# One block's second matrix products run as two half-height streams that trade accumulator banks

## The chip, the cores and the metric

The kernel runs on one core of a Trainium2 chip. The metric is the device time of one execution in microseconds (us), as the median of several runs. Beside it stands one profiled execution, with the start and duration of every instruction on each engine: TensorE (PE, its weight loads listed apart as PEld), VectorE (DVE), ScalarE (ACT), GpSimd (POOL) and SyncE (SP), which here issues every DMA.

## The reference

A decayed causal attention without softmax makes the activations `x`; a feed-forward layer with a rational activation follows.

```python
scores = (1 / sqrt(D)) * q @ k^T              # 8 batches, 8 heads, 576 positions, D = 64
ret = scores * where(rel >= 0, gamma ** rel, 0)
x = (ret @ v) as [4608 tokens, 512]
h = x @ w_in                                  # w_in 512 x 2048
g = (a0 + a1 h + a2 h^2 + a3 h^3) / (1 + |b0| |h| + |b1| h^2 + 1e-6)
out = g @ w_out                               # w_out 2048 x 512
```

## The kernel before, in words

The tokens are cut into nine blocks `b` of 512, the 2048 hidden channels into sixteen parts `f` of 128. A step is one pair `(b, f)`; there are 144 of them, and blocks 2 to 8 run one after the other with f = 0 to 15. Values that enter TensorE are split into a high and a low part (`xhi`, `xlo`; `g[:, 0]`, `g[:, 1]`; `w[:, 0]`, `w[:, 1]`), and of the four products of two split numbers three are made.

In each step TensorE does two things. `gemm1` makes the hidden values `h` of one part: 12 products of a 128x128 stationary operand with 512 moving columns, into one accumulator bank. `gemm2` adds one part's contribution to the block's output: for each of four token groups `t` of 128 tokens, three products with `g[:, i, ts]` stationary and the 512 columns of `w[:, j, :]` moving, all contracting over the full 128 channels. The four groups have a bank each, in two tiles `accs[b]` of two banks (`t // 2` is the tile, `t % 2` the bank), open over the block's 16 parts. `gemm2` runs three steps behind `gemm1`, since between them ScalarE and VectorE work out the rational function (`ffn_p` to `ffn_q3`) and split it (`ffn_hi`, `ffn_lo`).

Every fourth step also holds a `visit`: the attention of one 128-token unit, in products of 64 rows by 64 columns on quarters of TensorE's array. Its two halves of the array's rows run as two streams (`emit`) that write different accumulator banks. Where a half comes to a bank that the other half wrote before, `follow` makes it wait: an empty instruction on SP waits for the earlier product, and the later product waits for that instruction. After a visit SP issues the two 512 KB loads of a later unit (`load_unit`: `qk`, then `kv`).

The order on each engine is the order in which the code is written out (`InOrder`): lists of names per step, of which `REST` holds for this part of the program. In it `visit` comes behind `gemm1`, and `gemm2` behind `visit`. All compute instructions carry the line number of the helper that records them. In block 4, the fifth, the visits fall in the steps of which `gemm2` does parts 3, 7, 11 and 15; that of part 15 of block 3 comes just ahead of it.

Of the kernel before, what the change touches and what calls it, by code (L numbers as in the profile page):

```python
# [21 lines left out]
P = 128  # L22
B, H, S, D = 8, 8, 576, 64
# [31 lines left out]

VISITS = {0: (4, 5), 2: (5, 6), 4: (6, 7), 6: (7, None), 23: (None, 8)}
FIRST_DENSE = 22
VISITS |= {24 + 2 * i: (8 + i, 9 + i) for i in range(3)}
VISITS |= {30 + 4 * i: (11 + i, 12 + i if i < 24 else None) for i in range(25)}
WARM = [8, 3, 2]  # L60
# [16 lines left out]
def retention_ffn(ctx: ExitStack, tc: tile.TileContext, qkv, w_in, w_out, ab, masks, gq, gv, out):  # L77
# [10 lines left out]
    nc = tc.nc  # L88
# [15 lines left out]
    pe, act, dve, pool = (InOrder(tc, e) for e in (nc.tensor, nc.scalar, nc.vector, nc.gpsimd))  # L104
# [187 lines left out]
    def follow(ins, earlier):  # L292
        how = mybir.DependencyInfo(mybir.DependencyClass.Sync, mybir.DependencyReason.DATA)
        tc.add_manual_dep(ins.ins, earlier.ins.name, how, reason="rows of the array that write one bank")
        return ins
# [85 lines left out]
    accs = {}  # L381
# [68 lines left out]
    def ffn_lo(b, f, by_pool):  # L450
# [4 lines left out]
        else:  # L455
            dve.tensor_tensor(g[:, 1, :], p, g[:, 0, :].bitcast(F32), ALU.subtract)

    def gemm2(b, f, first, last):
        if first:
            accs[b] = [ps_acc.tile([P, 2, DM], F32, tag="acc", name=f"acc{b}_{f}_{t}") for t in range(2)]  # L460
        g = gs.pop((b, f))
        w = parts[1, f]
        for t in range(4):
            ts = slice(t * P, (t + 1) * P)
            acc = accs[b][t // 2][:, t % 2, :]
            for k, (i, j) in enumerate(((0, 0), (0, 1), (1, 0))):
                pe.matmul(acc, g[:, i, ts], w[:, j, :], start=(first and k == 0), stop=(last and k == 2))
        if not last:
            return
        for t, acc in enumerate(accs.pop(b)):  # L470
            r0 = b * 512 + t * 256
            rows = out[r0 : r0 + 256, :].rearrange("(t p) d -> p t d", p=P)
            if b == 1:
                for j in range(2):
                    o = cnv.tile([P, DM], F32, tag="c", name=f"o{b}_{t}_{j}")
                    act.activation(o, acc[:, j, :], AF.Copy, scale=-1.0)
                    nc.sync.dma_start(rows[:, j, :], o)
                continue
            if b == 0 and f == NF - 1:
                o = part[t]  # L480
                dve.scalar_tensor_tensor(o, acc, -1.0, o, ALU.mult, ALU.add)
            else:
                o = op.tile([P, 2, DM], F32, tag=f"o{t}", name=f"o{b}_{t}_{f}")
                act.activation(o, acc, AF.Copy, scale=-1.0)
            if f < NF - 1:
                part.append(o)
            else:
                nc.sync.dma_start(rows, o)
# [4 lines left out]
    first = half + NF  # L493
# [77 lines left out]
    def products(i):  # L571
        nonlocal done
        while done < len(steps) and i - done >= lag(i):
            gemm2(*steps[done])
            done += 1

    for i in range(len(steps) + lag(len(steps))):
# [3 lines left out]
        if i in VISITS:  # L581
            a, k = VISITS[i]
# [13 lines left out]
        if i == half:  # L596
            ps = ps_at.tile([P, 2, 512], F32, tag="at", name="free_at")
            free_at.extend((ps[:, 0], ps[:, 1]))
        elif i == FIRST_DENSE - 1:
            free_at.clear()  # L600
# [43 lines left out]
```

## Time and profile before

| | |
|---|---|
| median of 3 runs | 940.39 us (940.2 to 940.61) |
| profiled execution, whole | 940.24 us |
| its span, first to last instruction | 938.5 us |
| PE busy | 899.4 us (96%), 7852 products |
| DVE busy | 825.0 us (88%) |
| ACT busy | 710.2 us (76%) |
| POOL busy | 153.0 us (16%) |
| DMA | 65.50 MB, mean 70 GB/s |

Products overlap in TensorE's pipeline: the duration listed for one with 512 columns is 0.39 us, while the next one starts 0.23 us after it. What one costs in a row of them is therefore read from the distance of starts. Where a row stands for several instructions, its duration runs from the first one's start to the last one's end. The names `acc`, `h`, `ps`, `y`, `qk` and `kv` in the profile are the tiles of the code.

### The profile page before, as it was taken

How to read it: one execution, taken by the hardware profiler on the slowest of the kernel's cores; microseconds unless marked ns; L12 is line 12 of the kernel's file. 1: busy time of each engine (PE TensorE's matmuls, PEld its weight loads, DVE VectorE, ACT ScalarE, POOL GpSimd, SP SyncE). 2: the span in 40 equal slices, each digit the busy share in tenths (PEclk: the TensorE clock that was granted, in tenths of full speed). 3: DMA queues.
4: the chain of work that ended last, by engine and by line, in shares of the span. 5: the costliest groups of instructions: out<-in, count | busy, mean ns of one | idle time of the engine just before them, and what ended most of it. 6: DMA issues, size and time to landing. Idle time of an engine off the chain costs nothing.

```text
span 938.5 us, 19369 instructions
## 1 busy us (share of the span) xinstructions
PE 899.4 (96%) x7852; PEld 737.2 (79%) x7852; DVE 825.0 (88%) x1252; ACT 710.2 (76%) x1274; POOL 153.0 (16%) x128
## 2 busy tenths in 40 slices
PE   6689889989999999999999999999999999999997
PEld 6567668877878888888888888888888888888886
DVE  3799999999888888888888999898888888888895
ACT  4567788887777777877787778777877787867775
POOL 3544344444100000000000000000000000000000
PEclk9789999989999999999999999999999999999999
DMA  9976000003212111211121112111211121001001
GB/s 341 362 276 203 1 0 1 1 13 124 91 46 87 49 36 32 84 40 41 43 90 45 47 46 91 45 47 46 90 46 46 45 91 47 1 1 45 1 1 45
DMA packets 20568, 65.50 MB, mean 70 GB/s; under 512 B 2432, under 2 KB 2432, under 8 KB 20480
## 3 DMA queue, kind: packets, MB, share of 16 engines
q1 hardware_dynamic: 20480, 64.28, 19.5%
q8 instruction: 61, 1.00, 0.4%
q14 instruction: 27, 0.22, 0.1%
HBM read 54.83 MB, written 9.44 MB: 68 GB/s over the span
## 4 chain that ended last, share of the span: by engine, by line
PE 46%; DVE 28%; ACT 20%; issue 4%; DMA 1%; POOL 0%; SPq 0%; DVEq 0%; ACTq 0%; POOLq 0%
PE h L73 21%; PE acc L73 20%; DVE p L73 14%; DVE v L73 7%; ACT u L73 6%; ACT v L73 4%; ACT g L73 3%; ACT kv L73 3%; DVE c L73 3%; ACT free_at L73 2%; PE psNone L73 2%; PE ps L73 2%; DVE qk L73 1%; DVE g L73 1%; DVE xlo L73 1%
## 5 line engine op out<-in xcount | busy, mean ns | idle before, releaser
L73 PE MATMUL acc<-w,g 128*128 128x512 f32 x1632 | 399.7, 394 | 5.5 <-ACT o L73 3.6
L73 PE MATMUL h<-xhi,w 128*128 128x512 f32 x1152 | 385.4, 396 | 15.9 <-DVE p L73 15.9
L73 PEld LDWEIGHTS acc<-w,g 128*128 128x128 f32 x1632 | 305.4, 189 | 72.3 <-ACT o L73 4.0
L73 PEld LDWEIGHTS h<-xhi,w 128*128 128x128 f32 x1152 | 219.3, 190 | 69.0 <-DVE p L73 23.0
L73 PE MATMUL h<-xlo,w 128*128 128x512 f32 x576 | 227.0, 394 | 0.0
L73 ACT ACTIVATE p<-h,ab_sb 128x512 f32<-128x512 f32 x144 | 111.2, 772 | 74.8 <-PE h L73 69.6
L73 ACT ACTIVATE u<-h 128x512 f32<-128x512 f32 x131 | 78.0, 596 | 88.8 <-DVE v L73 88.3
L73 DVE SCALAR_TENSOR_TENSOR p<-p,ab_sb,u 128x512 f32<-128x512 f32 x131 | 120.1, 916 | 25.8 <-ACT u L73 20.4
L73 PEld LDWEIGHTS h<-xlo,w 128*128 128x128 f32 x576 | 109.7, 190 | 22.1
L73 DVE TENSOR_TENSOR v<-v,u 128x512 f32<-128x512 f32 x131 | 95.0, 725 | 28.5 <-ACT v L73 28.5
L73 DVE SCALAR_TENSOR_TENSOR p<-p,ab_sb,h 128x512 f32<-128x512 f32 x144 | 107.6, 747 | 4.7
L73 DVE TENSOR_TENSOR p<-p,h 128x512 f32<-128x512 f32 x144 | 98.9, 687 | 14.5 <-ACT u L73 14.2
L73 ACT ACTIVATE v<-u,absb 128x512 f32<-128x512 f32 x131 | 105.2, 803 | 0.5
L73 DVE SCALAR_TENSOR_TENSOR p<-v,p 128x512 f32<-128x512 f32 x144 | 99.6, 691 | 4.5
L73 POOL TENSOR_TENSOR S<-S,gv_sb 128x256 f32<-128x256 f32 x32 | 20.1, 628 | 483.7 <-DVE S L73 480.9
L73 ACT ACTIVATE u<-u,lnb 128x512 f32<-128x512 f32 x131 | 94.9, 724 | 4.3
L73 ACT ACTIVATE g<-p 128x512 fp32r<-128x512 f32 x136 | 85.8, 631 | 12.0 <-DVE p L73 5.4
L73 ACT ACTIVATE u<-v,lnb 128x512 f32<-128x512 f32 x131 | 93.3, 712 | 2.0 <-DVE v L73 2.0
L73 DVE SCALAR_TENSOR_TENSOR v<-v,u 128x512 f32<-128x512 f32 x131 | 91.7, 700 | 0.0
L73 DVE TENSOR_TENSOR g<-p,g 128x512 fp32r<-128x512 f32 x112 | 78.9, 704 | 1.4 <-ACT g L73 1.4
L73 ACT ACTIVATE kv<-kv,gv_sb 128x64 f32<-128x64 f32 x288 | 72.4, 334 | 9.8 <-DMA gv_sb<-in_gv 5.6
L73 POOL TENSOR_TENSOR qk<-qk,gq_sb 128x512 f32<-128x512 f32 x36 | 58.3, 1619 | 55.4 <-DMA qk<-in_qkv 55.4
(72 smaller groups left out, 726.1 us busy)
## 6 DMA issues: line engine op xcount, KB each, us to landing
qk<-in_qkv SPq DMA_DIRECT2D x36, 512.0 KB, 4.0
kv<-in_qkv SPq DMA_DIRECT2D x36, 512.0 KB, 5.6
bits<-in_w_in SPq DMA_DIRECT2D x16, 512.0 KB, 8.8
bits<-in_w_out SPq DMA_DIRECT2D x16, 512.0 KB, 8.2
out<-o SPq DMA_DIRECT2D x16, 512.0 KB, 3.4
out<-o SPq DMA_DIRECT2D x4, 256.0 KB, 2.3
gq_sb<-in_gq SPq DMA_DIRECT2D x1, 256.0 KB, 2.9
mask_sb<-in_masks SPq DMA_DIRECT2D x1, 32.0 KB, 5.1
```

The costliest lines, as they stand in the source:

```text
L73: return lambda *a, **k: self.tc.keep_in_program_order(method(*a, **k))
```

## The change

In block 4 `gemm2` calls a new function. Each product over 128 channels becomes two over 64: channels 0 to 63 on rows 0 to 63 of the array, channels 64 to 127 on rows 64 to 127. The two halves work side by side on two token groups and thus on two banks: groups (0, 1), then (2, 3), and then each half takes the other's groups, (1, 0) and (3, 2). A block's part so has 24 products in place of 12, as 12 pairs. With each third product of a half goes an empty instruction on SP, and a half that comes to a bank waits, by `follow`, for the one of the half that was there before.

```diff
+BY_ROWS = 4
...
+    ends = {}
+
+    def gemm2_by_rows(b, g, w, first, last):
+
+        begun = set()
+        for pair in ((0, 1), (2, 3), (1, 0), (3, 2)):
+            for k, (i, j) in enumerate(((0, 0), (0, 1), (1, 0))):
+                for row, t in enumerate(pair):
+                    r = slice(row * D, row * D + D)
+                    again = t in begun
+                    ins = pe.matmul(
+                        accs[b][t // 2][:, t % 2, :], g[r, i, t * P : (t + 1) * P], w[r, j, :],
+                        start=first and k == 0 and not again, stop=last and k == 2 and again, skip_group_check=True,
+                    )
+                    if k == 0 and t in ends:
+                        follow(ins, ends[t])
+                    if k == 2:
+                        ends[t] = follow(nc.sync.nop(), ins)
+            begun |= set(pair)
+
     def gemm2(b, f, first, last):
...
-        for t in range(4):
-            ts = slice(t * P, (t + 1) * P)
-            acc = accs[b][t // 2][:, t % 2, :]
-            for k, (i, j) in enumerate(((0, 0), (0, 1), (1, 0))):
-                pe.matmul(acc, g[:, i, ts], w[:, j, :], start=(first and k == 0), stop=(last and k == 2))
+        if b == BY_ROWS:
+            gemm2_by_rows(b, g, w, first, last)
+        else:
...
```

The first place is TensorE's queue around part 1 of block 4, a step without a visit; before, the end of part 4's `h` and the twelve products into the two `acc` tiles read so:

```order
L73 MATMUL h4_4_5137<-xhi4_4032,w0_4_680 128x512
L73 MATMUL acc4_0_0_5118<-w1_1_722,g4_1_5113 128x512 [waits Activation_49]
L73 MATMUL acc4_0_0_5118<-w1_1_722,g4_1_5113 128x512
L73 MATMUL acc4_0_0_5118<-w1_1_722,g4_1_5113 128x512 [waits DVE_49]
L73 MATMUL acc4_0_0_5118<-w1_1_722,g4_1_5113 128x512 x3
L73 MATMUL acc4_0_1_5119<-w1_1_722,g4_1_5113 128x512 x6
L73 MATMUL h4_5_5179<-xhi4_4032,w0_5_847 128x512
```

At the same place of TensorE's queue now:

```order
L74 MATMUL h4_4_5157<-xhi4_4032,w0_4_680 128x512
L74 MATMUL acc4_0_0_5118<-w1_1_722,g4_1_5113 128x512 [waits SP_sequencer_49,Activation_49]
L74 MATMUL acc4_0_0_5118<-w1_1_722,g4_1_5113 128x512 x3
L74 MATMUL acc4_0_0_5118<-w1_1_722,g4_1_5113 128x512 [waits DVE_49]
L74 MATMUL acc4_0_0_5118<-w1_1_722,g4_1_5113 128x512
L74 MATMUL acc4_0_1_5119<-w1_1_722,g4_1_5113 128x512 [waits SP_sequencer_49]
L74 MATMUL acc4_0_1_5119<-w1_1_722,g4_1_5113 128x512 x5
L74 MATMUL acc4_0_0_5118<-w1_1_722,g4_1_5113 128x512 [waits SP_sequencer_49]
L74 MATMUL acc4_0_0_5118<-w1_1_722,g4_1_5113 128x512 x5
L74 MATMUL acc4_0_1_5119<-w1_1_722,g4_1_5113 128x512 [waits SP_sequencer_49]
L74 MATMUL acc4_0_1_5119<-w1_1_722,g4_1_5113 128x512 x5
L74 MATMUL h4_5_5219<-xhi4_4032,w0_5_847 128x512
```

Each tile now comes twice, and each of the four groups of pairs begins with a wait for SP.

The second place is TensorE's queue where a visit has ended and part 3 follows; before:

```order
L73 MATMUL acc4_0_0_5118<-w1_3_1054,g4_3_5199 128x512 x2
L73 MATMUL acc4_0_0_5118<-w1_3_1054,g4_3_5199 128x512 [waits DVE_49]
L73 MATMUL acc4_0_0_5118<-w1_3_1054,g4_3_5199 128x512 x3
L73 MATMUL acc4_0_1_5119<-w1_3_1054,g4_3_5199 128x512 x6
L73 MATMUL h4_7_5343<-xhi4_4032,w0_7_1118 128x512 [waits DVE_49]
```

And the same place of TensorE's queue now:

```order
L74 MATMUL acc4_0_0_5118<-w1_3_1054,g4_3_5239 128x512 x4
L74 MATMUL acc4_0_0_5118<-w1_3_1054,g4_3_5239 128x512 [waits DVE_49]
L74 MATMUL acc4_0_0_5118<-w1_3_1054,g4_3_5239 128x512
L74 MATMUL acc4_0_1_5119<-w1_3_1054,g4_3_5239 128x512 x6
L74 MATMUL acc4_0_0_5118<-w1_3_1054,g4_3_5239 128x512 [waits SP_sequencer_49]
L74 MATMUL acc4_0_0_5118<-w1_3_1054,g4_3_5239 128x512 x5
L74 MATMUL acc4_0_1_5119<-w1_3_1054,g4_3_5239 128x512 [waits SP_sequencer_49]
L74 MATMUL acc4_0_1_5119<-w1_3_1054,g4_3_5239 128x512 x5
L74 MATMUL h4_7_5423<-xhi4_4032,w0_7_1118 128x512 [waits DVE_49]
```

Here the first two groups of pairs bring no wait of their own, since the visit's last wait for SP already covers them; the third and fourth wait for SP instructions that stand in SP's queue behind the loads which the visit sets off.

More of the change, by code (lines that the diff above doesn't have):

```diff
@@ L462, in gemm2 @@
         w = parts[1, f]
-        for t in range(4):
-            ts = slice(t * P, (t + 1) * P)
-            acc = accs[b][t // 2][:, t % 2, :]
-            for k, (i, j) in enumerate(((0, 0), (0, 1), (1, 0))):
-                pe.matmul(acc, g[:, i, ts], w[:, j, :], start=(first and k == 0), stop=(last and k == 2))
+        if b == BY_ROWS:
+            gemm2_by_rows(b, g, w, first, last)
+        else:
+            for t in range(4):
+                ts = slice(t * P, (t + 1) * P)
+                acc = accs[b][t // 2][:, t % 2, :]
+                for k, (i, j) in enumerate(((0, 0), (0, 1), (1, 0))):
+                    pe.matmul(acc, g[:, i, ts], w[:, j, :], start=(first and k == 0), stop=(last and k == 2))
         if not last:
```

## The prediction

> **What bounds the kernel now.** I read the page's busy shares first, then the stretch in which block 4's second products run (474 to 569 us) by engine, then the waits in that stretch, then TensorE's timeline. The page, then the stretch:
>
> ```profile
> PE 899.4 (96%) x7852; PEld 737.2 (79%) x7852; DVE 825.0 (88%) x1252; ACT 710.2 (76%) x1274; POOL 153.0 (16%) x128
> ...
> 474.00:569.00 95.00, 94.82 (x857) 77.48 (x856) 85.00 (x128) 73.22 (x133) 8.63 (x7) 1.00 0.15 51
> ```
>
> The second row's columns are PE, PEld, DVE, ACT and POOL. TensorE is busy for 94.82 of 95.00 us, at a granted clock of 1.00; VectorE, next, has 10 us to spare. The waits of the same stretch:
>
> ```profile
> PEld h L73 <- DVE p L73: 1.5, 4, 0.6
> PE h L73 <- DVE p L73: 0.2, 1, 0.2
> PEld acc L73 <- DVE g L73: 0.2, 1, 0.2
> ACT p L73 <- PE h L73: 4.5, 4, 1.4
> ```
>
> TensorE hardly waits, ScalarE waits for it. So TensorE's time here is the kernel's time: what the change adds to its queue moves the end, less the little that TensorE loses to VectorE today. The timeline of one step, second products, then `h`:
>
> ```profile
> 479.66 2.88 PE L73 MATMUL acc<-w,g 128*128 128x512 f32 x12
> 482.38 0.39 PE L73 MATMUL h<-xhi,w 128*128 128x512 f32 x1
> ...
> 485.10 2.88 PE L73 MATMUL acc<-w,g 128*128 128x512 f32 x12
> ```
>
> Twelve products take 482.38 - 479.66 = 2.72 us, 0.227 each, and the step 5.44 us, all of it products.
>
> **The pairs.** Each part's 12 products become 12 pairs. Whether a pair costs one product's time or two depends on the halves running at once. Before has such halves in the visits: `y` and `ps` are the two halves, `x2` the two column quarters of one.
>
> ```profile
> 467.64 0.22 PE L73 MATMUL y<-kv 64*64 64x64 f32 x2
> 467.66 0.23 PE L73 MATMUL ps<-kv 64*64 64x64 f32 x2
> 467.70 0.23 PE L73 MATMUL y<-kv 64*64 64x64 f32 x2
> 467.72 0.22 PE L73 MATMUL ps<-kv 64*64 64x64 f32 x2
> ...
> 491.86 0.34 PE L73 MATMUL ps<-kv 64*64 64x64 f32 x6
> ```
>
> With both halves at work a round takes 467.70 - 467.64 = 0.06. In the last row (a window that cuts it) one half works alone, three rounds of two: less the 0.22 of the last one, 0.12 for two steps, 0.06 each again. So the second half is free, and it writes another bank at the same time. I take 0.227 us per pair, nothing added to the 2.72 us of a part. What these rows don't show is two halves with 512 columns each and 128 output columns; bounds are 0.227 and 0.454 per pair, and I take the lower since the rows are of the same halves in the same kernel.
>
> The Trainium skill ("TensorE: Matmul & The Clock Gate", section "LDWEIGHTS (loading the stationary operand)") says that a weight load's time goes by its columns, not its rows; 24 half loads would then cost twice the 12 whole ones. By the load time found below (0.11) two of them one behind the other would be 0.22, still under a pair's 0.227, but 0.11 more at each of 16 entries, 1.8 us; by the rows of the visit, where four loads start together, nothing. I go by the rows.
>
> **Entry and exit.** TensorE now changes between whole-array and half-array products around every part. The visits show both directions:
>
> ```profile
> 490.31 0.39 PE L73 MATMUL h<-xhi,w 128*128 128x512 f32 x1
> 490.63 0.46 PE L73 MATMUL ps<-qk,kv 64*64 64x64 f32 x16
> 490.91 0.41 PE L73 MATMUL ps<-qk,S 64*64 64x64 f32 x16
> 491.15 0.41 PE L73 MATMUL ps<-qk,kv 64*64 64x64 f32 x16
> ...
> 466.65 0.41 PE L73 MATMUL ps<-qk,S 64*64 64x64 f32 x16
> ...
> 468.05 0.41 PE L73 MATMUL ps<-qk,kv 64*64 64x64 f32 x16
> 468.40 0.73 PE L73 MATMUL acc<-w,g 128*128 128x512 f32 x2
> ```
>
> Entry: the last `h` has its slot until 490.31 + 0.227 = 490.54; the visit starts at 490.63, 0.09 late, and its first sixteen take 0.28 where the next take 0.24, since their loads could not run ahead: 0.05. Together 0.14. Exit: the visit's slot ends at 468.05 + 0.24 = 468.29, the whole-array product's load starts at 468.40, 0.11 late, and the first two products span 0.73 in place of 0.39 + 0.227 = 0.62, 0.11 for the load that was not hidden. Together 0.22. A half product has 128 columns to load, as the exit has, so I take 0.22 for entry too. Twelve parts stand between two `h` groups: 12 x (0.22 + 0.22) = 5.3. Four parts follow a visit, whose exit becomes the entry to halves, one change for another: 4 x 0.22 = 0.9 for their exits alone. Sum 6.2 us. Lower end: entries at the visit's 0.14, 12 x 0.36 + 0.9 = 5.2. Upper end: two loads one after the other at each of 16 entries, 6.2 + 16 x 0.11 = 8.0.
>
> **The exchange of banks.** The third and fourth groups of pairs wait for SP's empty instruction behind the first and second. The visits have the same wait, and SP's instruction there:
>
> ```profile
> L290 SPq EVENT_SEMAPHORE  x1: 17/17/17, 492.1 to 492.1; - x1
> ...
> 491.98 0.40 PE L73 MATMUL ps<-kv 64*64 64x64 f32 x8
> 492.17 0.28 PE L73 MATMUL ps<-qk,kv 64*64 64x64 f32 x2
> ```
>
> SP's instruction (17 ns) is over at about 492.13 and the waiting product starts at 492.17; I take 0.1 us from a product's end to the load it releases. A group's last product starts at 2 x 0.227 = 0.45 after the group and ends 0.39 later, so the load is free at 0.94. It is due, one product ahead of its own, 5 x 0.227 = 1.13 after the group. It is 0.19 early: no cost where SP is free. Parts further on wait for what ended 2.72 us of `h` ago. If this cover went, each of 16 parts would show a late load, at least 0.11.
>
> SP is not free after a visit: its queue holds that visit's two load issues, and the empty instructions stand behind them.
>
> ```profile
> 492.81 0.35 SPq L116 DMA_DIRECT2D qk<-in_qkv  x1
> 493.28 1.55 SPq L118 DMA_DIRECT2D kv<-in_qkv  x1
> ...
> 517.30 0.47 SPq L118 DMA_DIRECT2D kv<-in_qkv  x1
> ...
> 541.44 0.86 SPq L118 DMA_DIRECT2D kv<-in_qkv  x1
> ...
> 565.98 0.89 SPq L118 DMA_DIRECT2D kv<-in_qkv  x1
> ```
>
> ```profile
> 492.66 3.02 PE L73 MATMUL acc<-w,g 128*128 128x512 f32 x12
> 495.58 0.50 PE L73 MATMUL h<-xhi,w 128*128 128x512 f32 x1
> 495.91 0.40 PE L73 MATMUL h<-xlo,w 128*128 128x512 f32 x1
> ...
> 516.66 3.02 PE L73 MATMUL acc<-w,g 128*128 128x512 f32 x12
> ...
> 540.82 3.02 PE L73 MATMUL acc<-w,g 128*128 128x512 f32 x12
> 544.02 0.50 PE L73 MATMUL h<-xhi,w 128*128 128x512 f32 x1 [0.18 <-DVE p L73]
> 544.36 0.39 PE L73 MATMUL h<-xlo,w 128*128 128x512 f32 x1
> ...
> 565.32 3.02 PE L73 MATMUL acc<-w,g 128*128 128x512 f32 x12
> ```
>
> The four parts' first products really begin 0.11 behind their rows' starts. From there SP ends its second issue after 2.06, 1.00, 1.37 and 1.44 us; 0.1 later the third group's load is released, which was due at 1.13: 1.03, 0, 0.34 and 0.41 late, and each late load shows its 0.11. Sum 2.1 us. Bounds: nothing if all four issues are as short as 0.47, 4 x (1.03 + 0.11) = 4.6 if all are as long as 1.55. Behind these nothing else on SP is hurried: block 3's output issues come before part 0, whose third group is the first to wait.
>
> **What TensorE stops losing.** After a visit `h` waits today for VectorE to free its bank. First row: the last of twelve starts at 492.66 + 3.02 - 0.39 = 495.29, the second `h` product was due 0.454 later, at 495.74, and starts at 495.91: 0.17. The third part gives 540.82 + 3.02 - 0.39 + 0.454 = 543.90 against 544.36, 0.46; the same reckoning at the other two gives 0.09 and 0.20. These 0.9 us run beside the new exits and late groups, and go. At least nothing of it goes, at most 0.9.
>
> **The sum.** 6.2 + 2.1 - 0.9 = 7.4 us on the profiled execution's 940.24 (span 938.5, 1.74 around it): 947.6. That execution is 0.15 below the median of the runs, which is left as it is. By its bounds this case runs from +4.3 (5.2 + 0 - 0.9) to +12.6 (8.0 + 4.6), 944.5 to 952.8. A measurement of this kernel can tell about 0.2%, 1.9 us, from no change.
>
> **Rivals.** (a) No change of mode costs anything, since both kinds of product load ahead into the rows that come free. The visits speak against it, but there the columns were split as well, and here only the rows are. Then 0 + 2.1 - 0.9 = +1.2, 941.4: no change.
>
> (b) Faster: as (a), SP's issues short, and a pair a little quicker than a whole product. The warm-up products bound that:
>
> ```profile
> 19.58 0.72 PE L73 MATMUL unread<-gq_sb 128*128 128x128 f32 x5
> ...
> 19.69 0.61 PE L73 MATMUL unread<-gq_sb 128*128 128x128 f32 x4
> ```
>
> One of these, 128 columns in two passes' time, takes 0.11; a visit's round of 64 such columns 0.058 (24 rounds from 466.65 to 468.05, the rows of the exit). The difference, 0.052 for 64, makes 8 x 0.052 / 2 = 0.208 for 512 single-pass columns, and 0.006 of fixed cost 0.214: 0.013 less than 0.227, over 192 pairs -2.5 us, 937.7. It decides only if 28 changes of mode cost under 0.09 each.
>
> (c) The halves take turns when each streams 512 columns, since the visits' two-pass products may leave the banks idle every other tick. Each pair then costs 0.227 more: 192 x 0.227 = 43.6, and 947.6 + 43.6 = 991. Against it stands the round of 0.06. The Trainium skill (the same page, section "Measured speedup vs the span model") has four row tiles of 32 rows and 512 columns 3.07 times as fast together; no run here shows that. If the missing part of 4, 4 / 3.07 = 1.30, fell on each pair, an estimate from that page would be 0.30 x 43.6 = 13 us more, 961.
>
> (d) SP's round trip is longer behind a 512-column product than behind a small one, by the 0.33 to 0.35 that SP takes over a short issue. Then the load is released at 1.29, 0.16 late, and shows 0.11: 0.27 in 12 parts, 3.2 us, 950.8; with every issue at 1.55 another 2.5, 953.3.
>
> **Chances.** The forecast 0.65, (a) 0.12, (b) 0.04, (c) 0.10, (d) 0.07, something else 0.02. The range leaves out (c) and the forecast's upper tip: 941 to 953. Slower by over 0.2%: the forecast, (c), (d), 0.82. Within 0.2%: (a) and the 0.02, 0.14. Faster by more: (b), 0.04.
>
> **What the profile after would show.** If I am right, TensorE has 8044 products; a part's 24 span about 2.72 us from first start to the exit, with starts in twos 0.227 apart; the first product after each change starts about 0.1 late and its successor another 0.11; in the four visit parts the third group is late by what SP's `kv` issue overran. Under (a) there are no gaps at the changes. Under (c) a part spans 5.4 us. Under (d) the third group is late in every part. A wrong price of the change of mode, which comes 28 times, would do most harm: 0.1 off is 2.8 us.

## The result, and the profile after

The kernel after takes 947.16 us (945.59 to 947.47), the kernel before, in the same comparison, 940.30 (940.04 to 940.61). The ratio is 1.0069, with an interval of 1.0052 to 1.0087: slower by 0.7%. The profiled execution took 947.47 us at a span of 945.7.

The busy row of the page after, and the row of the window view for block 4's second products (PE, PEld, DVE, ACT, POOL, then the granted clock):

```profile
PE 908.9 (96%) x8044; PEld 736.3 (78%) x8044; DVE 823.6 (87%) x1252; ACT 709.3 (75%) x1274; POOL 152.6 (16%) x128
...
474.00:576.00 102.00, 101.44 (x1048) 75.12 (x1047) 86.19 (x131) 72.80 (x133) 7.77 (x8) 1.00 0.14 47
```

There are 192 more products, and in the stretch TensorE is still busy almost throughout at a clock of 1.00, while VectorE has even more to spare. Busy time does not show the loss: a product is listed for 0.39 us or more, so a next start that comes 0.32 after it in place of 0.227 leaves no idle time. The distances of starts show it. To place it, I take the stage from the first product of block 3's part 15 to that of block 5's part 0. Its two ends in TensorE's timeline after:

```profile
468.54 1.66 PE L74 MATMUL acc<-w,g 128*128 128x512 f32 x6
...
578.62 1.75 PE L74 MATMUL acc<-w,g 128*128 128x512 f32 x7
```

and its end before (its start, 468.40, stands in the prediction):

```profile
571.11 2.88 PE L73 MATMUL acc<-w,g 128*128 128x512 f32 x12
```

So 110.08 us in place of 102.71: the stage costs 7.37. Ahead of it the two executions differ by 0.14, behind it 0.3 is won back. Two steps without a visit, in TensorE's timeline after:

```profile
474.10 0.39 PE L74 MATMUL h<-xhi,w 128*128 128x512 f32 x1
474.42 3.04 PE L74 MATMUL acc<-w,g 64*128 64x512 f32 x24
477.39 0.50 PE L74 MATMUL h<-xhi,w 128*128 128x512 f32 x1
477.72 0.40 PE L74 MATMUL h<-xlo,w 128*128 128x512 f32 x1
...
480.04 0.39 PE L74 MATMUL h<-xhi,w 128*128 128x512 f32 x1
480.35 3.04 PE L74 MATMUL acc<-w,g 64*128 64x512 f32 x24
```

The step is 480.35 - 474.42 = 5.93 us, before 5.44. It shows both kinds of change of mode. At entry the pairs start 0.32 after the last `h` product, where products elsewhere are 0.227 apart: 0.09 of standstill. At exit the last pair starts at 474.42 + 3.04 - 0.39 = 477.07, `h` follows after 0.32 and its second product after another 0.33: 0.09 of standstill and 0.10 for a load that nothing covered. A cut of the next part, by windows that end earlier, shows the same load at entry:

```profile
480.35 0.50 PE L74 MATMUL acc<-w,g 64*128 64x512 f32 x2
480.35 0.73 PE L74 MATMUL acc<-w,g 64*128 64x512 f32 x4
480.35 0.97 PE L74 MATMUL acc<-w,g 64*128 64x512 f32 x6
```

The first pair takes 0.50 in place of 0.39, and each further pair adds 0.23 to 0.24, not 0.45: the two halves do run side by side. The Trainium skill ("TensorEngine Tiling (Array Packing)", section "Key Properties") says that a change of the tiling mode drains TensorE. The trace agrees: the first row behind a change starts 0.32 after the last product and has 0.11 of load in it, so the product itself begins 0.43 after, just behind the 0.39 for which the last one is listed (an end that is modelled). Standstill and load together make some 0.2 us per change here.

The waits from 474 to 576 us (total us, times, longest; "issue" is idle time that no signal of another engine is seen to end):

```profile
PEld h L74 <- issue: 4.2, 12, 0.4
...
PEld acc L74 <- issue: 3.9, 11, 0.4
PEld acc L74 <- SPq L476: 2.2, 4, 0.7
```

Twelve of the sixteen exits and eleven of the twelve entries have rows of "issue", which did not stand there before; the other five have rows of the same 0.4 us under the names of other engines. VectorE's `p`, on which TensorE's loads for `h` waited before, is not among the rows of this stretch any more. The last row is new too: four waits for SP. They lie in the four visit parts:

```profile
494.25 1.66 PE L74 MATMUL acc<-w,g 64*128 64x512 f32 x12
496.19 1.66 PE L74 MATMUL acc<-w,g 64*128 64x512 f32 x12 [0.28 <-SPq L476]
...
520.29 3.21 PE L74 MATMUL acc<-w,g 64*128 64x512 f32 x24
...
546.17 1.66 PE L74 MATMUL acc<-w,g 64*128 64x512 f32 x12
548.11 1.64 PE L74 MATMUL acc<-w,g 64*128 64x512 f32 x12 [0.28 <-SPq L476]
...
572.47 3.33 PE L74 MATMUL acc<-w,g 64*128 64x512 f32 x24
```

with these issues of the second load on SP:

```profile
494.87 1.14 SPq L119 DMA_DIRECT2D kv<-in_qkv  x1
...
520.90 0.77 SPq L119 DMA_DIRECT2D kv<-in_qkv  x1
...
546.80 1.14 SPq L119 DMA_DIRECT2D kv<-in_qkv  x1
...
573.15 0.80 SPq L119 DMA_DIRECT2D kv<-in_qkv  x1
```

The first issue ends at 496.01 and the third group begins at 496.19, the third ends at 547.94 and the group begins at 548.11: 0.17 later, both times. The group was due 6 x 0.227 = 1.36 after its part's start (either row begins with 0.11 of load that nothing covers, so the two starts compare). From first start to last start the four parts take 3.21, 2.82, 3.19 and 2.93 us, where such a part takes 2.63 if nothing is late (the second experiment below): 0.58 + 0.19 + 0.56 + 0.30 = 1.6 us.

### The profile page after: what moved, and what is told of

It reads as the page before. It is cut to its first block, busy times and chain, and to the rows that moved or that the text cites. A ratio compares the mean times of both kernels' runs of the same rounds, so it can differ in the third digit from the quotient of the medians.

```text
span 945.7 us, 19890 instructions
## 1 busy us (share of the span) xinstructions
PE 908.9 (96%) x8044; PEld 736.3 (78%) x8044; DVE 823.6 (87%) x1252; ACT 709.3 (75%) x1274; POOL 152.6 (16%) x128
## 3 DMA queue, kind: packets, MB, share of 16 engines
q8 instruction: 63, 1.03, 0.5%
## 4 chain that ended last, share of the span: by engine, by line
PE 76%; DVE 11%; ACT 7%; issue 3%; DMA 2%; SPq 0%; POOL 0%; DVEq 0%; ACTq 0%
PE acc L74 35%; PE h L74 35%; DVE p L74 4%; DVE c L74 3%; PE ps L74 3%; DVE v L74 3%; ACT free_at L74 2%; PE y L74 2%; DMA qk<-in_qkv 1%; ACT v L74 1%; DMA kv<-in_qkv 1%; ACT u L74 1%; ACT g L74 1%; PE psNone L74 1%; ACT kv L74 1%
## 5 line engine op out<-in xcount | busy, mean ns | idle before, releaser
L74 PE MATMUL acc<-w,g 128*128 128x512 f32 (+1 forms) x1824 | 403.1, 396 | 5.3 <-ACT o L74 3.6
L74 PEld LDWEIGHTS acc<-w,g 128*128 128x128 f32 (+1 forms) x1824 | 304.3, 188 | 77.4 <-issue 4.7
L74 ACT ACTIVATE g<-p 128x512 fp32r<-128x512 f32 x136 | 85.7, 630 | 11.2 <-DVE p L74 5.4
```

Of the source, the lines that this page charges most:

```text
L74: return lambda *a, **k: self.tc.keep_in_program_order(method(*a, **k))
```

## The experiments

Each theory of the expectations is the forecast's sum, term by term. Stage differences below are those of the profiled executions against before, over the stage named above.

**SP's part.** Keep each half on its banks, so that nothing waits for SP:

```diff
-        for pair in ((0, 1), (2, 3), (1, 0), (3, 2)):
+        for pair in ((0, 1), (2, 3), (0, 1), (2, 3)):
...
-                    if k == 0 and t in ends:
-                        follow(ins, ends[t])
-                    if k == 2:
-                        ends[t] = follow(nc.sync.nop(), ins)
```

> Each half keeps its two banks (pairs (0, 1), (2, 3), (0, 1), (2, 3)), so no wait and no SP instruction is needed; half of the sum is left out and the other half made twice. All 192 pairs and 28 changes of mode stay. Theory (the changes of mode cost 0.2 us each, the exchange only what SP's loads hold up): the four late third groups of the changed kernel's profile, 1.54 us with their late loads, go, and up to 0.5 of VectorE's waits come back: 945.9 to 946.4. Rival (the exchange costs something in every part): under 945. Rival (pairs themselves are dear): no different from the theory here.

946.37 us (945.24 to 946.72), ratio 1.0057 (1.0044 to 1.0069); stage +5.77. Within the expectation.

Then the change itself, with the visits' loads written behind the step instead of inside it:

```diff
-            load_unit(a + 2)
+            (held.append if 20 < a + 2 < 26 else load_unit)(a + 2)
...
+        while held:
+            load_unit(held.pop(0))
```

> The changed kernel in full, but the loads that a visit sets off during block 4 are issued behind that step's second products, so SP is free for the exchange. Theory: as the kernel whose halves keep their banks, 945.9 to 946.4, no late third group in the visit parts. Rival (the exchange costs something in every part): over a microsecond above that kernel.

945.55 us (944.85 to 946.40), ratio 1.0050 (1.0036 to 1.0064), a touch under the expectation; stage +5.78. The visit parts of its timeline:

```profile
494.26 3.02 PE L74 MATMUL acc<-w,g 64*128 64x512 f32 x24
...
519.77 3.05 PE L74 MATMUL acc<-w,g 64*128 64x512 f32 x24
...
545.49 3.02 PE L74 MATMUL acc<-w,g 64*128 64x512 f32 x24
...
571.23 3.02 PE L74 MATMUL acc<-w,g 64*128 64x512 f32 x24
```

SP's issues in the first of these parts:

```profile
494.42 0.35 SPq L118 DMA_DIRECT2D qk<-in_qkv  x1
495.45 0.36 SPq L120 DMA_DIRECT2D kv<-in_qkv  x1
```

On SP the edit moved less than its text says: `qk` still comes ahead of the empty instructions, 0.16 after the part's start, and `kv` comes behind those of the first group of pairs, on which the third group waits, but not behind the others. In the last visit part `kv` kept its old place too. The `kv` issues were also shorter in this run, 0.33 to 0.64 us against 0.77 to 1.14 after, so the run does not tell the place from the length. Both runs lose no time to SP and land within 0.01 us of each other in the stage. So 7.37 - 5.78 = 1.6 us of the change are the waits for SP, which in the rows of after end 0.17 behind the `kv` issue, and the exchange by itself costs nothing where SP is free.

The counterpart has SP's waits without halves: whole products, of which those of the third and fourth token group wait for an instruction on SP behind the first and second.

```diff
-        for pair in ((0, 1), (2, 3), (1, 0), (3, 2)):
+        for t in (0, 1, 2, 3):
...
+                ins = pe.matmul(
+                    accs[b][t // 2][:, t % 2, :], g[:, i, t * P : (t + 1) * P], w[:, j, :],
+                    start=first and k == 0, stop=last and k == 2,
+                )
+                if k == 0 and t >= 2:
+                    follow(ins, ends[t - 2])
+                if k == 2:
+                    ends[t] = follow(nc.sync.nop(), ins)
```

> Whole products as before, but with the SP instructions and with the third and fourth group waiting for the first and second as in the exchange. No change of mode. Theory: nothing in the twelve parts without a visit; in the four others late groups of 1.5 us in all, of which VectorE's waits of 0.9 us there hide part: 940.8 to 941.8. Rival (the round trip through SP costs in every part): 943 or more.

941.12 us (940.08 to 941.83), ratio 1.0004 (0.9995 to 1.0012): not told from no change; stage +0.42. A visit part of its timeline:

```profile
492.37 1.66 PE L74 MATMUL acc<-w,g 128*128 128x512 f32 x6
494.46 1.66 PE L74 MATMUL acc<-w,g 128*128 128x512 f32 x6 [0.43 <-SPq L472]
```

The third group is due at 492.37 + 1.36 = 493.73 and starts 0.73 late; with two more, at 0.37 and 0.35, SP costs 1.45 us. That the stage grows by 0.42 alone shows the third term of the sum: behind the late groups VectorE is in time, and 1.03 us of waits for it go.

**The pairs.** Compute with one half of the rows alone:

```diff
-                for row, t in enumerate(pair):
+                for row, t in enumerate(pair[:1]):
```

(the waits and `begun` are taken out as well).

> The half on rows 64 to 127 is left out: a part has 12 products of 64 rows over channels 0 to 63, the other channels' share of the sum is missing, no exchange, no waits. Theory (the halves run side by side, the second one free): as with both halves and banks kept, 945.2 to 946.7. Rival (the second half takes some of the first one's time, about 4 ns of a pair's 231): 192 x 0.0045 = 0.9 lower, 944.3 to 945.5, with products 0.227 apart. Rival (the halves take turns): 43 us lower.

945.53 us (945.40 to 946.32), ratio 1.0055 (1.0043 to 1.0068); stage +5.37, 0.40 us less than the first experiment. The median fits the theory and lies at the edge of the first rival; the rows tell more. One step:

```profile
474.88 3.03 PE L74 MATMUL acc<-w,g 64*128 64x512 f32 x12
...
478.19 0.40 PE L74 MATMUL h<-xlo,w 128*128 128x512 f32 x1
...
480.47 0.39 PE L74 MATMUL h<-xhi,w 128*128 128x512 f32 x1
480.79 3.03 PE L74 MATMUL acc<-w,g 64*128 64x512 f32 x12
```

Twelve products of one half take what 24 of both take, 3.03 against 3.04. Nor are they 0.227 apart as the rival has them: from the first start to the last they take 3.03 - 0.39 = 2.64 us, and behind the first distance of 0.33 ten are left for 2.31. The 0.40 us do not lie in the pairs but in `h` behind them: its ten distances from 478.19 to 480.47 make 2.287 us (unrounded), against 2.313 with both halves, 0.03 less in each of 16 parts. So the pairs show no cost of a second half; were all of the 0.40 its own, it would be 2 ns for each of its 192 products. One half alone also starts 0.32 after the last `h`, as both do, and shows the same bare load: the second half's load adds none.

**The change of mode.** Half as many pairs at the same number of changes: groups 0 and 1 by halves, groups 2 and 3 whole.

```diff
-        for pair in ((0, 1), (2, 3), (1, 0), (3, 2)):
+        for n, what in enumerate(((0, 1), (0, 1), 2, 3)):
```

> Only groups 0 and 1 run as halves, without exchange and waits (half of their sum left out, the other half made twice); groups 2 and 3 run whole behind them. 28 + 0 changes of mode as in the changed kernel (two per part, one net in a visit's part), but 96 pairs in place of 192. Theory (price per change of mode): as with all four groups in halves and no exchange, 945.5 to 946.4. Rival (price per pair or per half product): half the loss, 943.0 to 943.4.

945.36 us (945.12 to 946.75), ratio 1.0051 (1.0039 to 1.0064); stage +5.32. This is 0.1 under what a price per change was expected to make, and 2 us over the rival by which the loss goes with the pairs: that one is out.

The same products with the whole groups between the halves, so that a part has four changes:

```diff
-        for n, what in enumerate(((0, 1), (0, 1), 2, 3)):
+        for n, what in enumerate(((0, 1), 2, (0, 1), 3)):
```

> Per part halves (0, 1), whole group 2, halves (0, 1) again, whole group 3: 96 pairs as with two groups in halves, but four changes of mode per part and three net in a visit's part, 60 in place of 28; half of the sum of groups 0 and 1 is left out. Theory (0.22 to 0.24 us per change): 940.4 + 60 x 0.22 to 0.24, less 0.9 of VectorE's waits: 952.7 to 953.9. Rival (price per pair): as with two groups in halves, 945.4.

952.11 us (950.84 to 952.64), ratio 1.0121 (1.0108 to 1.0135), slightly under the expectation; stage +11.94. One part of the one and of the other:

```profile
480.08 3.24 PE L74 MATMUL acc<-w,g 64*128 64x512 f32 x18
```

```profile
479.57 3.64 PE L74 MATMUL acc<-w,g 64*128 64x512 f32 x18
```

(The rows put halves and whole products together.) The two further changes inside a part cost 0.40, 0.20 each. Over the stages, 32 more changes cost 11.94 - 5.32 = 6.62, or 0.21 each.

**The distance of the exchange.** Let the halves trade banks after three pairs instead of six:

```diff
-        for pair in ((0, 1), (2, 3), (1, 0), (3, 2)):
+        for pair in ((0, 1), (1, 0), (2, 3), (3, 2)):
```

> The exchange comes at once: (0, 1), (1, 0), (2, 3), (3, 2), all computed. A group's load is released 0.45 + 0.39 + 0.1 = 0.94 us after the group ahead began and was due at 0.45: 0.49 late and 0.11 for the load, 0.6 twice a part, 19.2 us, and some 0.6 more in each part that follows a visit in place of the changed kernel's 1.5: 945.7 + 19.2 + 2.4 = 967. Rival (the halves' exchange is cheaper, since a product of 64 rows ends sooner than 0.39 us): each 0.05 us sooner is 1.6 us less. Rival (the wait has no effect on the time, the order alone guards the banks): 946.

963.31 us (961.85 to 964.64), ratio 1.0242 (1.0227 to 1.0257): a miss, the expectation was too high. One exchange, in its timeline cut after the fourth pair:

```profile
509.87 0.96 PE L74 MATMUL acc<-w,g 64*128 64x512 f32 x6
510.99 0.50 PE L74 MATMUL acc<-w,g 64*128 64x512 f32 x2 [0.16 <-SPq L476]
```

The fourth pair is due 3 x 0.227 = 0.68 after the first and comes after 1.12: 0.44 late in place of 0.60. The third pair ends at 509.87 + 0.96 = 510.83, and the fourth starts 0.16 later, by way of SP. The expectation called the load due a whole product, 0.227, ahead of its own and added its 0.11 on top, though 0.11 ahead is enough; and it took 0.1 for the way through SP in place of 0.16. Counted against the pair itself, 0.45 + 0.39 + 0.16 + 0.11 - 0.68 = 0.43. The forecast makes the same mistake (below). That the exchange after six pairs costs nothing is thereby bounded: it has 0.68 more, against 0.44 missing here.

**More of the same.** Six blocks by halves instead of one:

```diff
-BY_ROWS = 4
+BY_ROWS = range(2, 8)
...
-        if b == BY_ROWS:
+        if b in BY_ROWS:
```

> Blocks 2 to 7 all run by halves, everything computed. Theory (a price per change of mode): six times 6.8, 940.4 + 41 = 981, 979 to 983. Rival (part of the loss happens once, at the first block's start or by a shift of the loads): under 978.

987.16 us (984.89 to 987.70), ratio 1.0490 (1.0472 to 1.0507): 4 us above the expectation, so the loss comes with every block. With the loads written behind the step, as in the second experiment:

> Blocks 2 to 7 by halves, with the loads that the visits set off issued behind the step's second products. The blocks' parts without a visit cost the same 0.4 to 0.49 us each in all six blocks, so what differed between them should be SP's hold-ups. Theory: 6 x 6.0 to 6.3 over 940.4: 976.5 to 978.5, 9 to 10 us under the one with loads at once (987.2). Rival (later blocks cost more for another reason, such as VectorE's share of a visit): within 3 us of 987.

979.59 us (979.02 to 981.79), ratio 1.0417 (1.0402 to 1.0432): 1.1 above, but 7.6 under the one with the loads in the step. The waits of the first over blocks 2 to 7 (281 to 905 us), and of the second (280.5 to 897 us):

```profile
PEld h L74 <- issue: 26.9, 76, 0.4
PEld acc L74 <- issue: 24.5, 68, 0.9
PEld acc L74 <- SPq L476: 11.2, 16, 1.4
```

```profile
PEld h L74 <- issue: 26.1, 74, 0.4
PEld acc L74 <- issue: 24.5, 68, 0.9
...
PEld acc L74 <- SPq L477: 1.5, 3, 0.8
```

The rows of the changes of mode are nearly the same in both; the wait for SP falls from 11.2 to 1.5. So the miss was the term of SP again, this time too small: the loads' issues are longer in some blocks than in block 4 (up to 1.79 us), and a block costs between 6.0 and 9.1 us in the first run, 5.8 to 7.3 in the second. Why they are longer, I leave open, and so what still differs between the blocks of the second run.

**Fewer changes.** Do the second products of two parts in a row, so that block 4 has 12 changes in place of 28:

```diff
-        while done < len(steps) and i - done >= lag(i):
+        while done < len(steps) and i - done >= lag(i) + (steps[done][0] == 4 and steps[done][1] % 2 == 0):
```

> The changed kernel in full, but in block 4 an even part waits one step, so two parts' second products follow each other: 12 changes of mode in place of 28 (four pairs of parts between two h groups, four behind a visit). Theory (price per change): the same order with whole products + 12 x 0.21 to 0.24 + up to 1.5 for SP's loads: 943 to 944.5, if the order itself costs nothing. Rival (price per pair): no better than 947. Rival (24 h products in a row have to wait for VectorE to free h's banks): over 947, and the same loss with whole products.

943.65 us (943.13 to 945.21), ratio 1.0029 (1.0017 to 1.0042), as expected. Its control, the same order with whole products:

> The kernel before, with the same order of parts by twos in block 4 and whole products: the base for the one by halves. If the order costs nothing, 940 to 941; if h's products wait for VectorE, more, and the halves are to be compared with this.

940.45 us (940.16 to 941.54), ratio 0.9999 (0.9989 to 1.0008): the order costs nothing. Two parts of the one and of the other:

```profile
478.41 5.76 PE L74 MATMUL acc<-w,g 64*128 64x512 f32 x48
```

```profile
477.29 5.60 PE L73 MATMUL acc<-w,g 128*128 128x512 f32 x24
```

48 half products take 0.16 longer than 24 whole ones; the entry's standstill of 0.09 lies ahead of the row. Last, both remedies together:

> Two parts at a time by halves and the loads behind them, everything computed. Theory: the order by twos with whole products + 12 x 0.21 to 0.24, at most 0.5 us off for VectorE's waits: about 943, the least that halves cost here, still over the kernel before by 2 to 3. Rival (something apart from the changes and SP's loads): over 945.

942.79 us (941.92 to 943.78), ratio 1.0021 (1.0012 to 1.0030). This is the least of the versions run here that compute the whole result by halves, and still slower than before.

## Why the prediction was right

Forecast and result agree to 0.4 us (947.6 against 947.16), and the mechanism is the one forecast: the changes of mode carry the loss, SP's loads add to it, VectorE's waits give some back. Two terms were off, the changes 0.6 too low and SP 0.5 too high. That they cancel, and the sum is so close, is luck.

**The pairs** cost one product's time, as taken: 3.04 us for a part's 24 against 3.03 for one half's twelve. Rival (c), the halves in turns, is out by the run with one half alone, which is not 43 us faster. The Trainium skill ("TensorE: Matmul & The Clock Gate", section "LDWEIGHTS (loading the stationary operand)") says that a weight load takes its time by its columns, whatever the rows. The trace agrees: the bare load adds 0.11 to the first row at an entry, with 64 rows (0.50 in place of 0.39), and as much at an exit, with 128. What the forecast drew from this for its upper end, two loads of an entry one behind the other for another 0.11, did not come: with one half or with both the entry is the same, so here they go side by side.

**The changes of mode** were put at 0.22 each and 6.2 us in all. The stage without SP's waits grew by 5.78, while 1.04 of waits for VectorE went, so the 28 changes cost 6.8, 0.24 each. Standstill and uncovered load are 0.20 of it, read rightly from the visits; what the step left out is that the ten or so products behind a break are 0.231 apart on average in place of 0.227, another 0.04. Rival (a), changes that cost nothing, and with it (b) are out by the run with the banks kept and by the one with four changes in a part.

**SP** was put at 2.1 us and measured 1.6. The places and the cause were right. The step that was mis-sized is the loss of a late group: it called a load late from the slot one whole product ahead, at 1.13, and added its 0.11 on top. A load needs to be only its own 0.11 ahead of its product, which is due at 1.36; so 0.23 was counted too much. The way from SP to the group is 0.17 in place of the 0.1 taken. Counted as the forecast does from the part's first product, 0.11 behind its row's start, a group loses what issue end + 0.17 + 0.11 is beyond 1.36, which is 0.16 less than forecast for each of three late groups. With the issues of before that gives 0.98 + 0 + 0.29 + 0.36 = 1.6. After's own issues end 1.65, 1.27, 1.66 and 1.37 behind the first products: 0.57 + 0.19 + 0.58 + 0.29 = 1.6. That issues of other lengths add up to the same is chance.

**VectorE's waits** go, as foreseen: 1.04 against the 0.9 taken, since the wider spacing behind the break went with them. (From the start of a visit's last product to that of the next part's first, the four steps take, unrounded, 5.945, 5.845, 6.205 and 5.945 us before; where nothing waits, as in the first visit step of block 5 after, it is 5.725.) So 6.8 + 1.6 - 1.0 = 7.4.

**Not foreseen**: the first visit step of block 5, in which TensorE waits for VectorE before and does not after. Before:

```profile
589.54 3.02 PE L73 MATMUL acc<-w,g 128*128 128x512 f32 x12
...
595.39 0.84 PE L73 MATMUL acc<-w,g 128*128 128x512 f32 x3
```

After, with the first two and the last product of `h`:

```profile
597.04 3.02 PE L74 MATMUL acc<-w,g 128*128 128x512 f32 x12
599.90 0.39 PE L74 MATMUL h<-xhi,w 128*128 128x512 f32 x1
600.13 0.39 PE L74 MATMUL h<-xlo,w 128*128 128x512 f32 x1
...
602.39 0.39 PE L74 MATMUL h<-xhi,w 128*128 128x512 f32 x1
602.62 1.75 PE L74 MATMUL acc<-w,g 128*128 128x512 f32 x7
```

5.85 us before, 5.58 after: a block that delays TensorE seems to hand the next one a VectorE that is ahead. That is an argument, not a test: the step is 5.58 in every other run with block 4 alone by halves and with SP's waits on whole products, but 5.61 with whole products by twos, which cost no time. This makes most of the 0.3 behind the stage. Rival (d), a longer round trip behind a 512-column product, is out: only the visit parts have a late third group, and in the run with the exchange at once the round trip is 0.16. That is 0.06 over the 0.1 taken, which the cover of 0.19 holds.

## What to carry to other kernels

Two halves of the array's rows on separate banks run side by side at no extra time, but where the whole array would be filled they gain nothing, and each change between whole and part of the array costs about 0.2 us: put what runs in one mode together (12 changes in place of 28 took the loss from 0.7% to 0.3%). A wait that goes by way of a queue is as cheap as what stands ahead of it there: keep loads off that queue, or issue them behind, and look in the trace whether they went there. And count a late release once: add what the release takes and the bare load, and take as lost what lies beyond the time at which the product itself was due, not the lateness against an earlier slot with the load on top.

## What the runs showed of the hardware that was not expected

Products behind a break do not fall at once into their rhythm. In the step without a visit that stands first above, ten distances of `h` behind an exit, from 477.72 to 480.04, make 2.32 us; where nothing was held up, from 600.13 to 602.39, ten make 2.26. It wears off: with two parts at a time, 24 pairs in a row take 0.16 longer than 24 whole products, no more than the first bare load (0.11) and some ten wider distances (0.05). Why it is so, no run shows.

The way from the end of a product by way of an empty instruction on SP to the start of the row of a product that waits is 0.16 us, even behind products with 512 columns; the load of 0.11 at the head of that row comes on top.

The issue of a 512 KB load right behind another holds SP for anything from 0.33 us to 1.79, both in the run with six blocks:

```profile
589.24 0.33 SPq L119 DMA_DIRECT2D kv<-in_qkv  x1
...
640.65 1.79 SPq L119 DMA_DIRECT2D kv<-in_qkv  x1
```
